# Attention's TensorE work in five pieces a unit from the 17th head on, and the first two weight slices converted in the first batch with GpSimd

## The chip, the cores and the metric

The kernel runs on one core of a Trainium2 chip. The metric is device time of one execution in microseconds (us). The core has TensorE (PE, matmul), VectorE (DVE), ScalarE (ACT), GpSimd (POOL) and SyncE (SP, which issues the DMAs). Each engine works through its own instructions strictly in the order in which they were written, and an instruction whose input is not there holds up all that stand behind it on that engine.

## The reference

Softmax attention with a soft cap over 4 batches of 12 heads (448 tokens, head size 64), then layer norm, a two-layer perceptron (768 to 3072 to 768) and a residual.

```python
scores = cap * np.tanh(scale * np.matmul(q, k.transpose(0, 1, 3, 2)) / cap)   # 4 x 12 heads, 448 x 448
attn = np.exp(scores - np.max(scores, axis=-1, keepdims=True))
attn = attn / (np.sum(attn, axis=-1, keepdims=True) + 1e-09)
x = np.matmul(attn, v)                       # heads side by side: 4 x 448 x 768
xn = (x - mu) / np.sqrt(var + 1e-06) * g_ln
out = x + np.maximum(xn @ w_ch1, 0.0) @ w_ch2   # 768 x 3072, 3072 x 768; weights come as float64
```

## The kernel before

The kernel writes its whole instruction list through a planner of its own. `add` records a piece of work with its engine, a modelled cost, what it reads and writes, and a due time. `emit` then walks a modelled clock: whenever an engine is free in the model, it writes the ready piece with the earliest due time whose buffers are free. The order on each engine is therefore fixed when the program is built, by modelled costs; on the chip only the waits remain.

Attention is done in units of four heads (`quad`, 12 units, two head pairs each). Per unit TensorE has these slots, all in float32: six score slots (L534, two matmuls each: one key tile of 128 for both heads of a pair), one slot for the last 64 keys of all four heads (L545), two slots for the products with v (L428, six matmuls for one pair), one for the last 64 keys' part (L437) and one for the sums of the exponentials (L481, with a column of ones). In the trace each of these matmuls leaves two records. Behind them come transposes of the sums (L493) and of the outputs (L507). ScalarE takes tanh (L558) and exp (L562, L567). VectorE adds up exponentials over key tiles (L413, L415, L420), copies outputs and sums out of PSUM in the first batch (L452; ScalarE does it in the others, L450), forms and multiplies with the reciprocal sums (L496, L499, L517).

The perceptron (FFN) runs over 24 slices of 128 hidden columns. Token tiles are in groups: A0 (3 tiles), A1 (3), then C0 and C1 (8 tiles together), which come last. `up` (L756 to L758) and `down` (L781 to L783) do three float32r matmuls for each product: high by high, high by low, low by high. A0 can begin when the first 12 heads are done and normalized (L651 to L685); from then on TensorE's order mixes FFN matmuls and the attention slots of the units left.

Each slice has two weights, which arrive as float64 bits and are converted in six steps: DMA (L704), exponent scaled into `c` (L709, ScalarE), sign kept in `raw` (L711, GpSimd), two shift-and-or steps (L714, L716, VectorE), rounding into the high part `h` (L364, ScalarE), the low part `l` (L371, VectorE). No conversion begins before `self.late`, the last-keys product (L437) of the second unit. The first two `raw` buffers hold the keys and queries of the first unit before they take weights.

The lines the prediction uses most, beside these: the DMAs of v (L401) and of keys and queries (L387), issued by SP in one order with L704.

Of the kernel before, what the change touches and what calls it, by code (L numbers as in the profile page):

```python
# [66 lines left out]
    w1=20000, w2=3000, evac=2000, cstep=15600, cnorm=10000, load=20000, zpad=3000,  # L67
# [31 lines left out]
class Order:  # L99
# [34 lines left out]
    def emit(self, realize):  # L134
# [29 lines left out]
        while pending:  # L164
            done = False
            for e in free:
# [127 lines left out]
class Program:  # L294
# [79 lines left out]
    def quad(self, i, at):  # L374
# [32 lines left out]
        (self.scores_general if self.general else self.scores)(es, er, kqs, dues)  # L407
# [15 lines left out]
        pos = [buf("ps", "o", [128, 512], F32) for _ in range(2)]  # L423
        for p, e1 in enumerate(es):
            def pv(e, p=p, e1=e1):
                for j in range(NK):
                    for k in range(2):
                        nc.tensor.matmul(pos[p].ap[k * D:k * D + D, :S], lhsT=v.ap[:, (2 * p + k) * NK + j],  # L428
                                         rhs=e1.ap[:, k, j], start=(j == 0), stop=False)

            add({"T": 200 + NK * F4(S)}, pv, reads=[*v_all, (e1, 0), (e1, 1)], writes=[pos[p]], allocs=pos, due=dues[p] - PLAN["pv"])

        def pv_rest(e):
            for k in range(2):
                for p in range(2):
                    rows = slice(p * REST, p * REST + REST)
                    nc.tensor.matmul(pos[p].ap[k * D:k * D + D, :S], lhsT=v.ap[rows, 4 * NK + k],  # L437
                                     rhs=er.ap[rows, k], start=False, stop=True)

        self.last_pv = add({"T": 100 + F4(S)}, pv_rest, reads=[*v_all, er], writes=pos, due=dues[2] - PLAN["pv"])  # L440
# [5 lines left out]
        self.finish(i, ots, s1s, dues[2])  # L446
# [23 lines left out]
    def finish(self, i, pairs, parts, due):  # L470
# [6 lines left out]
        ps = buf("ps", "s", [128, 512], F32)  # L477

        def sums(e):
            for c in range(GROUP):  # L480
                nc.tensor.matmul(ps.ap[32 * c:32 * c + 32, :S], lhsT=self.ones, rhs=parts[c // 2].ap[:, c % 2],  # L481
                                 start=True, stop=True)

        add({"T": 200 + F4(S)}, sums, reads=parts, writes=[ps], due=due)
# [39 lines left out]
    def products(self, kqs, l, r, due, into, allocs):  # L524
# [3 lines left out]
        for p, kq in enumerate(kqs):  # L528
            for j in range(NK):
                zs = [self.buf("ps", "z", [128, 512], F32) for _ in range(2)]  # L530

                def qk(e, j=j, kq=kq, zs=zs):
                    for k, z in enumerate(zs):
                        self.nc.tensor.matmul(z.ap[:, :S], lhsT=kq.ap[rows[k], l, 128 * j:128 * j + 128],  # L534
                                              rhs=kq.ap[rows[k], r], start=True, stop=True)

                self.add({"T": 200 + F4(S)}, qk, reads=[(kq, 0), (kq, 1)], writes=zs, allocs=[allocs[p]], due=due[p] - PLAN["qk"])
                for k, z in enumerate(zs):
                    into(p, k, j, z)
# [383 lines left out]
```

## Time and profile before

| | |
|---|---|
| runs of the kernel before | 931.88, 933.9, 935.34 us; median 933.9 |
| profiled execution | 934.28 us, of which the span of instructions is 932.5 us |
| TensorE busy | 912.0 us of the span, granted clock 0.994 on average |
| VectorE, ScalarE, GpSimd busy | 610.5, 400.5, 134.0 us |
| first FFN matmul | starts 86.49 us into the span |

Times within the profile count from the span's start. PEclk is the granted clock of TensorE as a share of 2.4 GHz. A row of a timeline joins instructions of one line that follow each other; the bracket at its end gives the idle time before it and the instruction that ended that.

### The profile page before, as it was taken

How to read it: one execution, taken by the hardware profiler on the slowest of the kernel's cores; microseconds unless marked ns; L12 is line 12 of the kernel's file. 1: busy time of each engine (PE TensorE's matmuls, PEld its weight loads, DVE VectorE, ACT ScalarE, POOL GpSimd, SP SyncE). 2: the span in 40 equal slices, each digit the busy share in tenths (PEclk: the TensorE clock that was granted, in tenths of full speed). 3: DMA queues.
4: the chain of work that ended last, by engine and by line, in shares of the span. 5: the costliest groups of instructions: out<-in, count | busy, mean ns of one | idle time of the engine just before them, and what ended most of it. 6: DMA issues, size and time to landing. Idle time of an engine off the chain costs nothing.

```text
span 932.5 us, 12642 instructions
## 1 busy us (share of the span) xinstructions
PE 912.0 (98%) x4854; PEld 745.3 (80%) x4854; DVE 610.5 (65%) x900; ACT 400.5 (43%) x569; POOL 134.0 (14%) x224
## 2 busy tenths in 40 slices
PE   8998999899999999999999999999999999999997
PEld 4335766677877778779989998989889889899897
DVE  2698887878777667577898373837483482573622
ACT  6896596765555635653243131212150340330300
POOL 0023211312111101012621010100010120110100
PEclk9999999999999999999999999999999999999999
DMA  4765364444453434227234130402142241250112
GB/s 99 197 176 151 116 187 129 141 136 151 137 159 116 133 92 138 84 86 242 103 100 155 49 129 8 135 1 89 68 166 68 68 167 37 68 179 26 69 52 87
DMA packets 51158, 104.74 MB, mean 112 GB/s; under 512 B 28048, under 2 KB 34704, under 8 KB 51088
## 3 DMA queue, kind: packets, MB, share of 16 engines
q1 hardware_dynamic: 51088, 103.84, 36.2%
q8 instruction: 40, 0.66, 0.3%
q14 instruction: 30, 0.25, 0.1%
HBM read 95.16 MB, written 8.65 MB: 111 GB/s over the span
## 4 chain that ended last, share of the span: by engine, by line
PE 82%; DVE 8%; ACT 2%; POOL 2%; issue 1%; SPq 1%; DMA 1%; DVEq 0%; POOLq 0%; ACTq 0%
PE bank L756 12%; PE bank L781 11%; PE bank L758 11%; PE bank L757 11%; PE bank L783 11%; PE bank L782 11%; PE bank L428 4%; PE bank L534 4%; DVE x L785 2%; DVE raw L714 1%; SPq L401 1%; DVE st L651 1%; PE bank L507 1%; DVE c L716 1%; DVE l L371 1%
## 5 line engine op out<-in xcount | busy, mean ns | idle before, releaser
L781 PE MATMUL bank<-h,hh 128*128 128x384 f32 x672 | 226.0, 336 | 0.3 <-ACT e L558 0.3
L783 PE MATMUL bank<-h,hl 128*128 128x384 f32 x672 | 224.8, 335 | 0.6 <-DVE hl L763 0.6
L782 PE MATMUL bank<-l,hh 128*128 128x384 f32 x672 | 224.6, 334 | 0.0
L785 DVE TENSOR_TENSOR x<-bank,x 128x384 f32<-128x384 f32 x272 | 146.5, 551 | 113.7 <-PE bank L783 112.1
L711 POOL TENSOR_SCALAR raw<-raw 128x768 f32<-128x768 f32 x96 | 98.0, 1022 | 632.3 <-ACT c L709 618.4
L364 ACT ACTIVATE h<-c 128x768 fp32r<-128x768 f32 x96 | 81.0, 846 | 179.7 <-PE bank L783 123.1
L761 ACT ACTIVATE hh<-bank 128x384 fp32r<-128x384 f32 (+1 forms) x96 | 52.3, 545 | 198.7 <-PE bank L758 198.4
L781 PEld LDWEIGHTS bank<-h,hh 128*128 128x128 f32 x672 | 126.1, 188 | 7.9 <-ACT e L558 2.3
L783 PEld LDWEIGHTS bank<-h,hl 128*128 128x128 f32 x672 | 126.1, 188 | 0.9 <-DVE hl L763 0.9
L782 PEld LDWEIGHTS bank<-l,hh 128*128 128x128 f32 x672 | 126.2, 188 | 0.2
L714 DVE SCALAR_TENSOR_TENSOR raw<-raw 128x768 int32<-128x768 int32 x96 | 94.5, 986 | 41.3 <-POOL raw L711 41.0
L709 ACT ACTIVATE c<-raw 128x768 f32<-128x768 f32 x96 | 87.7, 917 | 76.0 <-DVE l L371 37.9
L756 PE MATMUL bank<-hC,h 128*128 128x512 f32 x288 | 114.0, 396 | 0.0
L758 PE MATMUL bank<-hC,l 128*128 128x512 f32 x288 | 113.8, 395 | 0.0
L757 PE MATMUL bank<-lC,h 128*128 128x512 f32 x288 | 113.7, 395 | 0.0
L371 DVE TENSOR_TENSOR l<-c,h 128x768 fp32r<-128x768 f32 x96 | 92.4, 963 | 28.6 <-ACT h L364 28.2
L763 DVE SCALAR_TENSOR_TENSOR hl<-bank,hh 128x384 fp32r<-128x384 f32 (+1 forms) x96 | 59.4, 618 | 67.9 <-ACT hh L761 67.7
L756 PE MATMUL bank<-hA,h 128*128 128x384 f32 x288 | 101.7, 353 | 0.0
L758 PE MATMUL bank<-hA,l 128*128 128x384 f32 x288 | 97.5, 339 | 0.5 <-DVE l L371 0.5
L757 PE MATMUL bank<-lA,h 128*128 128x384 f32 x288 | 97.5, 338 | 0.0
L716 DVE SCALAR_TENSOR_TENSOR c<-c,raw 128x768 int32<-128x768 int32 x96 | 95.0, 991 | 1.9
L558 ACT ACTIVATE e<-bank,sc 128x448 f32<-128x448 f32 x144 | 81.9, 643 | 15.9 <-PE bank L534 15.6
(75 smaller groups left out, 935.2 us busy)
## 6 DMA issues: line engine op xcount, KB each, us to landing
raw<-in_w_dram SPq DMA_DIRECT2D x96, 768.0 KB, 4.4
d<-in_kq_dram SPq DMA_DIRECT2D x44, 224.0 KB, 5.0
out_dram<-x SPq DMA_DIRECT2D x28, 192.0 KB, 1.9
d<-in_v_dram SPq DMA_DIRECT2D x96, 48.0 KB, 3.8
x<-xd SPq DMA_DIRECT2D x8, 384.0 KB, 5.8
xd<-a SPq DMA_DIRECT2D x21, 128.0 KB, 4.5
raw<-in_kq_dram SPq DMA_DIRECT2D x4, 224.0 KB, 4.1
d<-in_v_dram SPq DMA_DIRECT2D x48, 16.0 KB, 2.6
```

Source lines behind the costliest of these rows:

```text
L371: self.eng(e).tensor_tensor(out=out, in0=in_, in1=high.bitcast(F32), op=ALU.subtract)
L709: add({"A": ACTS(DM)}, lambda e: nc.scalar.activation(f(c.ap), f(hi()), AF.Copy, scale=2.0 ** -112), reads=[raw], writes=[c], due=due, aft ...
L711: add(on("sg", G=POOL1(DM), V=VEC1(DM)), lambda e: nc.gpsimd.tensor_scalar(f(hi()), f(hi()), 0.0, 1.0, op0=ALU.mult, op1=ALU.mult) if e == ...
L714: add({"V": VEC2(DM)}, lambda e: nc.vector.scalar_tensor_tensor(hi(), lo(), 29, hi(), op0=ALU.logical_shift_right, op1=ALU.bitwise_or), wr ...
L716: add({"V": VEC2(DM)}, lambda e: nc.vector.scalar_tensor_tensor(c.ap, c.ap, 3, hi(), op0=ALU.logical_shift_left, op1=ALU.bitwise_or), read ...
L756: nc.tensor.matmul(ps.ap[:, :n], lhsT=w1h.ap[:, wc], rhs=xh.ap[:, c], start=(c == 0), stop=False)
L757: nc.tensor.matmul(ps.ap[:, :n], lhsT=w1h.ap[:, wc], rhs=xl.ap[:, c], start=False, stop=False)
L758: nc.tensor.matmul(ps.ap[:, :n], lhsT=w1l.ap[:, wc], rhs=xh.ap[:, c], start=False, stop=(c == CC - 1))
L781: nc.tensor.matmul(o, lhsT=h[0].ap[:, mc], rhs=w[0].ap[:, hc], start=(f == 0), stop=False)
L782: nc.tensor.matmul(o, lhsT=h[0].ap[:, mc], rhs=w[1].ap[:, hc], start=False, stop=False)
L783: nc.tensor.matmul(o, lhsT=h[1].ap[:, mc], rhs=w[0].ap[:, hc], start=False, stop=(f == last))
L785: add({"V": VEC2(HALF)}, lambda e, t=t, ps=ps, hc=hc: nc.vector.tensor_tensor(out=self.x(t)[:, hc], in0=ps.ap[:, :HALF], in1=self.x(t)[:, ...
```

## The change

Three things change. First, from head index 16 on (units 5 to 12) a unit's eleven slots are recorded as five pieces that nothing can be put between: three score pieces of two slots each, one piece of the last-keys slot with the first pair's value product, and one piece of the second pair's value product, the last-keys product and the sums. The first four units keep single slots. The sums' due time is no longer put back by 9 us, in any unit. Second, the first two slices of weights (four conversions) no longer wait for `self.late`, are due 20 us earlier, and have their scaling and rounding (the steps of L709 and L364) on GpSimd, beside the sign step that was there. Third, the planner's model of TensorE's clock counts long pieces over several windows.

```diff
 WEIGHTS = [
-    dict(sg='G', h='A', l='V'),
-    dict(sg='G', h='A', l='V'),
-    dict(sg='G', h='A', l='V'),
+    dict(c='G', sg='G', h='G', l='V'),
+    dict(c='A', sg='G', h='A', l='V'),
 ]
-EARLY = 12
+EARLY = 2
+FINE = 16
 PLAN = dict(
-    ... load=20000, zpad=3000,
+    ... load=20000, zpad=3000, ahead=20000,
 # emit(): the model of TensorE's clock
-                        cold, busy, window = busy < (0.8 if cold else 0.4) * WINDOW, 0.0, window + WINDOW
+                        now = min(busy, WINDOW)
+                        cold, busy, window = now < (0.8 if cold else 0.4) * WINDOW, busy - now, window + WINDOW
 # quad()
-        (self.scores_general if self.general else self.scores)(es, er, kqs, dues)
+        qk_rest = (self.scores_general if self.general else self.scores)(es, er, kqs, dues, 1 if i < FINE else 2)
+        merged = i >= FINE and not self.general
+        if merged:
+            qk_rest(cost, lambda: pv(0), [*v_all, *done(0)], pos)
+        elif not self.general:
+            qk_rest()
...
+        if merged:
+            ps = self.sums(s1s, dues[2], cost + F4(S), lambda: (pv(1), pv_rest()), [*v_all, *done(1), er], pos)
+        else:
+            for p in range(2):
+                add({"T": 200 + cost}, lambda e, p=p: pv(p), reads=[*v_all, *done(p)], writes=[pos[p]],
+                    allocs=pos, due=dues[p] - PLAN["pv"])
+            add({"T": 100 + F4(S)}, lambda e: pv_rest(), reads=[*v_all, er], writes=pos, due=dues[2] - PLAN["pv"])
+            ps = self.sums(s1s, dues[2])
 # sums(), out of finish(): was due=due with PLAN["fin"] added
+            if first:
+                first()
+            for c in range(GROUP):
+                self.nc.tensor.matmul(ps.ap[32 * c:32 * c + 32, :S], lhsT=self.ones, rhs=parts[c // 2].ap[:, c % 2],
+                                      start=True, stop=True)
 # products()
+        slots = [(p, j) for p in range(2) for j in range(NK)]
+        for n in range(0, len(slots), at_once):
+            now = slots[n:n + at_once]
+            zs = [[self.buf("ps", "z", [128, 512], F32) for _ in range(2)] for _ in now]
...
+        def rest(cost=0, then=None, reads=(), writes=()):
...
+                if then:
+                    then()
 # weight()
-        part = WEIGHTS[2 if g else fc >= EARLY]
+        early = g == 0 and fc < EARLY
+        part = WEIGHTS[not early]
+        due -= PLAN["ahead"] * early
...
-        add({"A": ACTS(DM)}, lambda e: nc.scalar.activation(f(c.ap), f(hi()), AF.Copy, scale=2.0 ** -112),
-            reads=[raw], writes=[c], due=due, after=[self.late])
+        add(on("c", A=ACTS(DM), G=POOL1(DM)), lambda e: nc.scalar.activation(
+            f(c.ap), f(hi()), AF.Copy, scale=2.0 ** -112) if e == "A" else nc.gpsimd.tensor_scalar(
+            f(c.ap), f(hi()), 2.0 ** -112, 1.0, op0=ALU.mult, op1=ALU.mult),
+            reads=[raw], writes=[c], due=due, after=[] if early else [self.late])
```

In the order of TensorE, place one is the last unit (heads 45 to 48), amid FFN matmuls. Before, the last-keys product (L437) and the sums (L481) stand apart, and so does L428, just ahead of these rows:

```order
L437 MATMUL bank_208<-d_225,d_288 64x448
L437 MATMUL bank_229<-d_225,d_288 64x448
L437 MATMUL bank_208<-d_225,d_288 64x448
L437 MATMUL bank_229<-d_225,d_288 64x448
L756 MATMUL bank_230<-hA_692,h_67 128x384
L757 MATMUL bank_230<-lA_706,h_67 128x384
L758 MATMUL bank_230<-hA_692,l_69 128x384
L756 MATMUL bank_230<-hA_692,h_67 128x384
L757 MATMUL bank_230<-lA_706,h_67 128x384
L758 MATMUL bank_230<-hA_692,l_69 128x384
L481 MATMUL bank_218<-d_265,ones 32x448 x2
L481 MATMUL bank_218<-d_216,ones 32x448 x2
```

After (L415 is L428 of before, L422 is L437, L491 is L481, L796 to L798 are L756 to L758):

```order
L415 MATMUL bank_208<-e_282,d_270 64x448 x6
L422 MATMUL bank_230<-d_265,d_270 64x448
L422 MATMUL bank_208<-d_265,d_270 64x448
L422 MATMUL bank_230<-d_265,d_270 64x448
L422 MATMUL bank_208<-d_265,d_270 64x448
L491 MATMUL bank_219<-d_323,ones 32x448 x2
L491 MATMUL bank_219<-d_182,ones 32x448 x2
L796 MATMUL bank_200<-hA_1501,h_67 128x384
L797 MATMUL bank_200<-lA_1513,h_67 128x384
L798 MATMUL bank_200<-hA_1501,l_69 128x384
```

The six FFN matmuls that stood between the slots have moved out; the slots follow one another directly.

Place two is VectorE's order in the first unit, behind the last addition of exponentials (`d_248`, `d_288` are the sums of the two pairs; `b_184`, `b_186` take the outputs, `b_190` the sums; `raw` and `c` belong to the weights). Before:

```order
L420 TENSOR_TENSOR d_248<-d_248,d_272 64x896
L420 TENSOR_TENSOR d_288<-d_288,d_272 64x896
L452 COPY b_184<-bank_208 128x448
L452 COPY b_186<-bank_209 128x448
L452 COPY b_190<-bank_229 128x448
L413 TENSOR_TENSOR d_182<-e_282 128x896
L415 TENSOR_TENSOR d_182<-d_182,e_282 128x896
L496 TENSOR_SCALAR r_365<-bank_229,eps 128x16
```

After (L444 is L420, L466 is L452, L754 is L714, L756 is L716, L373 is L371, L437 and L439 are L413 and L415, L515 is L496):

```order
L444 TENSOR_TENSOR d_248<-d_248,d_272 64x896
L444 TENSOR_TENSOR d_288<-d_288,d_272 64x896
L754 SCALAR_TENSOR_TENSOR raw_63<-raw_63 128x768
L466 COPY b_184<-bank_208 128x448
L466 COPY b_186<-bank_209 128x448
L756 SCALAR_TENSOR_TENSOR c_65<-c_65,raw_63 128x768
L466 COPY b_190<-bank_199 128x448
L754 SCALAR_TENSOR_TENSOR raw_64<-raw_64 128x768
L373 TENSOR_TENSOR l_69<-c_65,h_67 128x768
L437 TENSOR_TENSOR d_182<-e_282 128x896
L515 TENSOR_SCALAR r_364<-bank_230,eps 128x16
L439 TENSOR_TENSOR d_182<-d_182,e_282 128x896
```

Two shift-and-or steps of the first weight now stand ahead of the copy into `b_190`, the first of them ahead of all three copies; a step of the second weight and the first low part follow at once.

Place three is TensorE at the same time, from the first unit's sums to the transposes of `b_190`. Before:

```order
L481 MATMUL bank_229<-d_248,ones 32x448 x2
L481 MATMUL bank_229<-d_288,ones 32x448 x2
L428 MATMUL bank_230<-e_282,d_225 64x448 x6
L534 MATMUL bank_209<-d_261 128x448
L534 MATMUL bank_199<-d_261 128x448
L493 MATMUL bank_229<-ident,b_190 128x128 x4
```

After (L512 is L493, L555 is L534):

```order
L491 MATMUL bank_199<-d_248,ones 32x448 x2
L491 MATMUL bank_199<-d_288,ones 32x448 x2
L555 MATMUL bank_200<-d_261 128x448
L555 MATMUL bank_218<-d_261 128x448
L555 MATMUL bank_219<-d_261 128x448
L555 MATMUL bank_229<-d_261 128x448
L512 MATMUL bank_230<-ident,b_190 128x128 x4
L415 MATMUL bank_208<-e_282,d_225 64x448 x6
```

The transposes of `b_190` have moved ahead of the second unit's first value product (L428, now L415).

## Rows read from the trace of the kernel before

**Rows 1.** The page, part 1: busy us (share of the span) xinstructions.

```profile
PE 912.0 (98%) x4854; PEld 745.3 (80%) x4854; DVE 610.5 (65%) x900; ACT 400.5 (43%) x569; POOL 134.0 (14%) x224
```

**Rows 2.** Busy time by stretch: us, each engine busy (x), PEclk, DMA share, GB/s.

```profile
26.22:33.75 7.53, 7.26 (x39) 2.23 (x33) 3.96 (x5) 5.67 (x8) 0.00 (x0) 1.00 1.03 303
33.75:81.27 47.52, 41.30 (x208) 15.49 (x206) 40.40 (x63) 41.94 (x57) 14.17 (x33) 1.00 0.67 165
80.80:84.30 3.50, 2.97 (x14) 2.97 (x15) 3.50 (x5) 2.28 (x4) 0.06 (x1) 0.51 0.80 242
171.60:184.10 12.50, 9.54 (x49) 8.15 (x48) 10.68 (x16) 8.29 (x12) 6.48 (x13) 0.86 0.17 55
200.00:435.00 235.00, 235.00 (x1342) 182.51 (x1341) 168.92 (x246) 131.91 (x192) 29.20 (x40) 1.00 0.42 127
```

**Rows 3.** Timeline of PE in the FFN: start, us, engine, line, operation, count.

```profile
309.50 1.77 PE L534 MATMUL bank<-d 64*128 64x448 f32 x8
...
311.20 0.44 PE L756 MATMUL bank<-hA,h 128*128 128x384 f32 x1
...
312.19 0.34 PE L758 MATMUL bank<-hA,l 128*128 128x384 f32 x1
...
312.46 1.02 PE L534 MATMUL bank<-d 64*128 64x448 f32 x4
...
313.41 0.44 PE L756 MATMUL bank<-hA,h 128*128 128x384 f32 x1
...
313.69 0.34 PE L757 MATMUL bank<-lA,h 128*128 128x384 f32 x1
```

**Rows 4.** Timeline of PE in the first batch, to the first FFN matmul.

```profile
11.77 4.96 PE L428 MATMUL bank<-e,d 128*64 128x448 f32 x12 [1.93 <-ACT e L562]
...
29.50 0.96 PE L481 MATMUL bank<-d,ones 128*32 128x448 f32 x8
...
30.39 2.48 PE L428 MATMUL bank<-e,d 128*64 128x448 f32 x12
...
33.75 0.66 PE L493 MATMUL bank<-ident,b 128*128 128x128 f32 x4
...
81.33 3.36 PE L676 MATMUL bank<-ident,xn 128*128 128x128 f32 x16 [2.65 <-DVE xn L668]
...
86.49 0.44 PE L756 MATMUL bank<-hA,h 128*128 128x384 f32 x1
```

**Rows 5.** Timeline of SP, and line L704 in the window 27.4 to 27.9.

```profile
27.44 0.99 SPq L704 DMA_DIRECT2D raw<-in_w_dram  x2
...
DMA to landing us min/median/max: 6.0/6.0/6.0
```

**Rows 6.** Timeline of DVE in the first batch.

```profile
26.72 1.16 DVE L452 COPY b<-bank 128x448 f32<-128x448 f32 x2 [0.50 <-PE bank L437]
...
62.00 1.62 DVE L714 SCALAR_TENSOR_TENSOR raw<-raw 128x768 int32<-128x768 int32 x1
...
64.94 0.97 DVE L714 SCALAR_TENSOR_TENSOR raw<-raw 128x768 int32<-128x768 int32 x1
...
80.07 1.20 DVE L668 TENSOR_SCALAR xn<-x,mv 128x768 f32<-128x768 f32 x1 [0.91 <-POOL mv L665]
```

**Rows 7.** Timeline of POOL in the first batch.

```profile
61.94 0.88 POOL L711 TENSOR_SCALAR raw<-raw 128x768 f32<-128x768 f32 x1 [3.21 <-ACT c L709]
```

**Rows 8.** Groups by form: line engine op | busy, mean ns | idle before.

```profile
L413 DVE TENSOR_TENSOR d<-e 128x896 f32<-128x896 f32 x24 | 26.0, 1083 | 29.5 <-ACT e L562 29.4
...
L415 DVE TENSOR_TENSOR d<-d,e 128x896 f32<-128x896 f32 x24 | 26.7, 1114 | 0.2
...
L420 DVE TENSOR_TENSOR d<-d,d 64x896 f32<-64x896 f32 x24 | 29.3, 1220 | 7.0 <-ACT d L567 6.6
...
L709 ACT ACTIVATE c<-raw 128x768 f32<-128x768 f32 x96 | 87.7, 917 | 76.0 <-DVE l L371 37.9 <-DMA raw<-in_w_dram 33.1 <-DVE x L785 4.3
...
L364 ACT ACTIVATE h<-c 128x768 fp32r<-128x768 f32 x96 | 81.0, 846 | 179.7 <-PE bank L783 123.1 <-DVE c L716 39.2 <-PE bank L757 17.1
```

More of the change, by code (lines that the diff above doesn't have):

```diff
@@ L421, in quad @@
                 out=s1.ap[rows], in0=s1.ap[rows], in1=er.ap[rows], op=ALU.add), reads=[er], writes=[s1], due=dues[2])
-        ots = []
[L423 to L440, printed above, removed]
+        if merged:
+            ps = self.sums(s1s, dues[2], cost + F4(S), lambda: (pv(1), pv_rest()), [*v_all, *done(1), er], pos)
+        else:
+            for p in range(2):
+                add({"T": 200 + cost}, lambda e, p=p: pv(p), reads=[*v_all, *done(p)], writes=[pos[p]],
+                    allocs=pos, due=dues[p] - PLAN["pv"])
+            add({"T": 100 + F4(S)}, lambda e: pv_rest(), reads=[*v_all, er], writes=pos, due=dues[2] - PLAN["pv"])
+            ps = self.sums(s1s, dues[2])
+        ots = []
         for p in range(2):
@@ L468, in token_tiles, with sums, finish @@
         return [(j, t + j, slice(0, 128) if j else slice(64, 128)) for j in range(4)]
-    def finish(self, i, pairs, parts, due):
+    def sums(self, parts, due, cost=0, first=None, reads=(), writes=()):
+        ps = self.buf("ps", "s", [128, 512], F32)
+        def sums(e):
+            if first:
[3 more added lines that the diff above has]
+                                      start=True, stop=True)
+        self.last_pv = self.add({"T": 200 + F4(S) + cost}, sums, reads=[*parts, *reads], writes=[ps, *writes], due=due)
+        return ps
+    def finish(self, i, pairs, ps, due):
         nc, add, buf = self.nc, self.add, self.buf
@@ L476, in finish @@
         due += PLAN["fin"] if h0 + GROUP < H else 0
[L477 to L484, printed above, removed]
         ss, d0 = self.out_tile("ss", i, due)
@@ L540, in products @@
-        zs = [self.buf("ps", "z", [128, 512], F32) for _ in range(2)]
-        def qk(e):
-            for p, kq in enumerate(kqs):
-                for k, z in enumerate(zs):
-                    self.nc.tensor.matmul(z.ap[p * REST:p * REST + REST, :S], lhsT=kq.ap[rows[k], l, 128 * NK:],
-                                          rhs=kq.ap[rows[k], r], start=True, stop=True)
-        self.add({"T": 200 + F4(S)}, qk, reads=[(kq, k) for kq in kqs for k in range(2)], writes=zs, allocs=[allocs[2]], due=due[2] - PLAN["qk"])
@@ L549, in products, with scores @@
-        for k, z in enumerate(zs):
-            into(2, k, 0, z)
-    def scores(self, es, er, kqs, due):
+                if then:
+                    then()
+            self.add({"T": 200 + F4(S) + cost}, qk, reads=[(kq, k) for kq in kqs for k in range(2)] + list(reads),
+                     writes=[*zs, *writes], allocs=[allocs[2]], due=due[2] - PLAN["qk"])
+            for k, z in enumerate(zs):
+                into(2, k, 0, z)
+        return rest
+    def scores(self, es, er, kqs, due, at_once):
@@ L581, in into @@
                 reads=[z], writes=[tiles[p]], due=due[p])
-        self.products(kqs, 1, 0, due, into, tiles)
+        self.products(kqs, 1, 0, due, into, tiles, at_once)()
         for p, (t, m) in enumerate(zip(tiles, ms)):
```

53 lines of the change are left out of this document (38 added, 15 removed).

## The prediction

> **What bounds the kernel now.** I read the page's shares first, then busy time by stretch, then single rows of TensorE, and from the waits of TensorE back to the engine that it waits for. TensorE is busy for 98% of the span [rows 1]. From 200 to 435 us, where FFN matmuls and attention alternate, it is busy for all 235 us at full clock, while VectorE works 168.9 us and ScalarE 131.9 [rows 2]: there a microsecond less of TensorE is a microsecond less of time, as long as no new wait comes. The first 86.5 us, up to the first FFN matmul [rows 4], are another stage. Between 33.75 and 81.27 us TensorE shows 41.3 of 47.5 us, but part of that is matmuls stretched by waits; ScalarE has 41.9 and VectorE 40.4 us, so VectorE is idle for 7.1 us [rows 2]. The reader should see that three engines share the bound in this stage, and that it ends with the norm of the first tokens: TensorE waits 2.65 us for VectorE's last normalized tile [rows 4], which ends at 80.07 + 1.20 = 81.27 us [rows 6]. The change saves in the second stage and rearranges the first.
>
> **Joining slots: minus 3.9 us.** In the FFN a joined pair of score slots (x8) starts at 309.50 and the next matmul at 311.20: 1.70 us. A lone slot (x4) goes from 312.46 to 313.41: 0.95 us. Joining two therefore saves 2 x 0.95 - 1.70 = 0.20 us. The FFN pays too: from 312.19 the slot's start is 0.27 us away, and the first FFN matmul behind it lasts 0.28 us to the next (313.41 to 313.69), while FFN matmuls follow one another at 0.174 us (from 311.20 to 312.19 there are five such steps, one of 0.28 and four of 0.174). So each stretch of FFN matmuls between two attention slots costs 0.10 + 0.11 = 0.21 us [rows 3]. Now I count in the two orders, from the first FFN matmul on: runs of score slots go from 34 to 23, stretches of FFN matmuls from 57 to 49; runs of the other slots stay as many, since a value product and the sums differ in shape and I let each keep its own start. 11 x 0.20 + 8 x 0.21 = 2.2 + 1.7 = 3.9 us. That is small, because the old order had already joined many slots by chance. The unit's pieces can add waits: a score piece wants four PSUM banks at once and the value product now stands right behind the last-keys slot. The pieces leave at least two FFN stretches between a score piece and its product, and ScalarE has 103 us free of 235 [rows 2], so I cost this at nothing; if the cover is gone, it can eat the 3.9 us, not much more.
>
> **Sums of the fourth unit: minus 0.9 us behind the first FFN matmul.** Their slot takes 30.39 - 29.50 = 0.89 us [rows 4] and moves ahead of it, where a lone score slot leaves its place in the last stretch before the FFN.
>
> **The early weights: plus 6.0 us at the first FFN matmul.** ScalarE is relieved: up to the fourth unit's last exp it loses three scalings of 0.917 and four roundings of 0.846 us [rows 8], 6.1 us in all. ScalarE is only one of three engines here, and the order of VectorE has to be read against SP. SP issues the DMAs of v, keys and queries first, in the same order as before, and reaches the first weight at 27.44 us; it lands 6.0 us later, at 33.4 [rows 5]. Then come two GpSimd steps of about 1 us (0.88 in [rows 7]), so the sign step ends at 35.4. VectorE's first shift-and-or waits for that, and in the new order it stands ahead of the first unit's three copies, which begin at 26.72 before [rows 6]. Behind it now: 0.97 for itself, 1.16 for two copies [rows 6], 0.97 for the second step and 0.6 for the last copy, in all 3.7 us: the copy of the sums ends near 39.0. TensorE's transposes (L493), 33.75 before [rows 4], start at 39.1, and in the new order the second unit's value product stands behind them. TensorE has nothing to do from about 29.5 us on, and ScalarE, which needs the next scores, soon runs dry as well. So the stage is 39.1 - 33.75 = 5.35 us late at this point.
>
> How much returns? From the transposes to the end of the last normalized tile before, VectorE is busy 40.4 us of 47.5 [rows 2]. The new order has the same fourteen weight steps in this stretch, and besides two L413, two L415 and one L420 of VectorE that stood outside: 2 x 1.083 + 2 x 1.114 + 1.220 = 5.6 us by the means [rows 8], 5.1 us when 0.1 each is taken off for their overlap with the next. What VectorE's idle time becomes no row shows: at least none of the 7.1 us, at most all. The tile ends between 39.1 + 40.4 + 5.1 = 84.6 and 91.7 us. I take half, 3.5 us, since the wait for ScalarE shrinks but the waits for transposes and for GpSimd's chain stay: 88.1, or 6.8 us later than 81.27. From there to the first FFN matmul before took 86.49 - 81.27 = 5.2 us, of which 80.8 to 84.3 went at a granted clock of 0.51 after TensorE's wait (1.2 instead of 2.4 GHz) [rows 2]; that half speed costs up to 1.7 us. More work stands close ahead now, so it may be spared; I take half, 0.8. That is +6.0 us, between +1.6 (84.6 and the whole 1.7) and +10.4. The idle 9.6 us also lower the clock at 39 us, as 1.93 idle us did before the value product that took 4.96 us where another takes 2.48 [rows 4]; this falls within the idle time counted.
>
> Does less conversion remain afterwards? At the first FFN matmul the same four low parts are done as before, so no slice comes earlier relative to TensorE.
>
> **The second norm: minus 1.9 us.** Around the second norm of 3 tiles, 171.6 to 184.1 us, TensorE is idle for 12.5 - 9.5 = 3.0 us and its mean clock is 0.86, which is another 1.7 [rows 2]. Between the last output transposes and the norm's the old order has 21 FFN matmuls, three lone score slots and a value product: 21 x 0.174 + 3 x 0.95 + 2.4 + 0.4 for the edges = 9.3 us. The new one has 33 FFN matmuls, a joined pair, a last-keys slot (taken as long as the sums) and a value product: 5.7 + 1.7 + 0.9 + 2.4 + 0.5 = 11.2 us. The 1.9 us more cover as much of the wait. Bounds: nothing, or all 4.7 us. The third norm and the end keep their order nearly unchanged: nothing.
>
> **Sum.** On the profiled execution: 934.3 + 6.0 - 0.9 - 3.9 - 1.9 = 933.6 us. This execution stands 0.4 us above the median of 933.9, which I leave out as smaller than the rest. I predict 934 us. The likeliest case by itself spans 930 to 938.
>
> **A rule that speaks against the change.** The row first: a GpSimd sign step ran from 61.94 to 62.82 [rows 7], and the VectorE step that started at 62.00 took 1.62 us instead of 0.97 [rows 6], 0.65 more. The Trainium skill, "SBUF — State Buffer", section "Who interferes with whom", says that VectorE with two SBUF inputs and a GpSimd instruction that reads SBUF exclude each other for a whole instruction. The trace agrees, with 0.65 us; by that rule eight more GpSimd steps in a busy VectorE stage would make the slower case below.
>
> **Rivals.**
> 1. *GpSimd holds VectorE up in the first batch: slower.* Eight added GpSimd steps fall between 33 and 56 us, where VectorE is now the fullest engine. If each costs it 0.65 us [rows 6, 7], the stage loses 5.2 us more: 6.0 + 5.2 = 11.2, and the time is 934.3 + 11.2 - 6.7 = 938.8, or 941 if more of VectorE's idle time stays than the half I took. For it: the pair of rows, and that low parts wait for GpSimd's rounding. Against: in many cases it is GpSimd that waits, and its chain has slack. It decides from a first FFN matmul at 97.5 us on (86.5 + 11.0, by which the sum passes 938.6).
> 2. *VectorE fills all its idle time: faster.* Then the first FFN matmul is 1.6 us late, and with 1.9 to 4.7 us from the second norm the time is 934.3 + 1.6 - 0.9 - 3.9 - 1.9 = 929.2 down to 926.4; I put 928. For it: ScalarE is relieved by 6.1 us, and it ended most of VectorE's idle time at L413 [rows 8]. Against: at the end of the stage the norm's chain through GpSimd leaves VectorE waiting in any order (0.91 us before its last tile [rows 6]).
> 3. *The change does not do what it says:* joined pieces stand together but TensorE waits within them for banks or exp, and the 3.9 us go into waits: 934.3 + 6.0 - 0.9 - 1.9 = 937.5.
>
> **How the numbers follow.** Likeliest case 0.54, rival 1 0.20, rival 2 0.18, rival 3 0.08. A measurement of this kernel can tell about 0.5% from no change, that is 4.7 us: faster is below 929.2, slower above 938.6. Rival 2 lies below (0.18) with 0.03 from the likeliest case; rival 1 lies above with 0.03 from the likeliest case and 0.03 from rival 3: faster 0.21, same 0.53, slower 0.26. The range reaches to both outer rivals: 927 to 941.
>
> **What would show it.** Right: TensorE waits some 9 us for VectorE's copy ahead of the first unit's L493 transposes, near 30 to 39 us; VectorE stands idle from 26 to 35 us until GpSimd's first sign step; the first FFN matmul at 90 to 95 us; from then on TensorE's record free of new waits, with score pieces of 1.70 us. Wrong: a first weight that lands well before 33 us; a first FFN matmul ahead of 86.5 us, which would give the early weights their gain; or value products with waits of a microsecond in the FFN stage.

## The result and the profile after

| | before | after |
|---|---|---|
| median of the runs taken together | 933.46 us | 942.94 us |
| profiled execution | 934.28 us | 943.18 us |
| its span of instructions | 932.5 us | 941.3 us |
| first FFN matmul starts | 86.49 us | 97.17 us |
| from there to the last matmul's end | 840.7 us | 836.9 us |
| from VectorE's last result to the end of the span | 4.7 us | 6.7 us |

The changed kernel is slower: ratio 1.010, 95% interval 1.0081 to 1.0120. The forecast was 934 with a range of 927 to 941, and the likeliest case was no change. The table splits the 8.8 us between the two spans: +10.7 up to the first FFN matmul, -3.9 from there to the last matmul, +2.0 behind it. TensorE's busy time in the middle part fell by 5.7 us, and its idle time rose by 1.9 (before, then after; us, then busy us of PE, PEld, DVE, ACT, POOL, then granted clock, DMA share, GB/s):

```profile
86.49:927.21 840.72, 836.27 (x4496) 712.77 (x4494) 552.43 (x808) 331.28 (x472) 118.52 (x178) 1.00 0.34 108
```

```profile
97.17:934.02 836.85, 830.54 (x4490) 712.13 (x4486) 546.03 (x806) 332.58 (x474) 118.61 (x178) 1.00 0.34 107
```

TensorE in the first batch of the changed kernel (start, us, line, operation, count, idle time before and what ended it), the answer to [rows 4]:

```profile
27.90 1.77 PE L555 MATMUL bank<-d 64*128 64x448 f32 x8
39.64 1.09 PE L512 MATMUL bank<-ident,b 128*128 128x128 f32 x4 [9.96 <-DVE b L466]
40.66 4.18 PE L415 MATMUL bank<-e,d 128*64 128x448 f32 x12
...
93.13 0.66 PE L712 MATMUL bank<-ident,xn 128*128 128x128 f32 x4 [1.50 <-DVE xn L704]
...
97.17 0.45 PE L796 MATMUL bank<-hA,h 128*128 128x384 f32 x1
```

The wait of 9.96 us ahead of the transposes (L512, L493 before) is the one that the prediction described. GpSimd's first two steps and VectorE behind them:

```profile
33.66 0.87 POOL L748 TENSOR_SCALAR c<-raw 128x768 f32<-128x768 f32 x1 [28.20 <-DMA raw<-in_w_dram]
34.62 0.86 POOL L751 TENSOR_SCALAR raw<-raw 128x768 f32<-128x768 f32 x1
```

```profile
35.51 0.96 DVE L754 SCALAR_TENSOR_TENSOR raw<-raw 128x768 int32<-128x768 int32 x1 [8.83 <-POOL raw L751]
...
38.88 0.61 DVE L466 COPY b<-bank 128x448 f32<-128x448 f32 x1
...
47.17 1.41 DVE L536 TENSOR_TENSOR x<-bank,r 128x256 f32<-128x256 f32 x4 [2.50 <-PE bank L526]
...
92.39 0.68 DVE L704 TENSOR_SCALAR xn<-x,mv 128x768 f32<-128x768 f32 x1 [0.65 <-POOL mv L701]
```

The weight lands at 33.5 us, the sign step ends at 35.5, the copy of the sums at 39.5. ScalarE, whose next scores stand behind the transposes on TensorE, runs dry in turn:

```profile
45.83 1.16 ACT L589 ACTIVATE e<-bank,sc 128x448 f32<-128x448 f32 x2 [13.47 <-PE bank L555]
```

Stretches of the changed kernel (us, then busy us of PE, PEld, DVE, ACT, POOL, then granted clock): the 10 us around the end of the wait, the stage from the transposes to the last normalized tile, and the second norm, which answers to the fourth row of [rows 2].

```profile
33.90:44.10 10.20, 4.46 (x14) 1.95 (x16) 8.59 (x12) 0.00 (x0) 5.02 (x7) 0.50 0.56 146
39.64:93.07 53.43, 46.59 (x226) 17.54 (x226) 46.18 (x67) 35.50 (x48) 22.49 (x37) 0.93 0.64 170
186.00:198.50 12.50, 9.66 (x60) 6.18 (x59) 11.14 (x16) 7.89 (x14) 4.01 (x11) 1.00 0.26 79
```

After the wait TensorE runs at 1.2 instead of 2.4 GHz (0.50), so the value product at 40.66 takes 4.18 us; before, the one at 30.39 took 2.48. The second norm runs at full clock, with 2.8 us idle.

What VectorE waited for in this stage (us in total, times, longest), after and then before:

```profile
DVE x L536 <- PE bank L526: 3.0, 2, 2.5
DVE xn L704 <- POOL mv L701: 1.6, 2, 0.9
DVE d L437 <- ACT e L593: 1.5, 1, 1.5
DVE l L373 <- POOL h L370: 0.7, 1, 0.7
```

```profile
DVE raw L714 <- POOL raw L711: 2.1, 2, 1.3
DVE xn L668 <- POOL mv L665: 1.6, 2, 0.9
DVE r L496 <- PE bank L493: 1.0, 1, 1.0
DVE x L517 <- PE bank L507: 0.8, 1, 0.8
```

The old waits for the sign steps (2.1 us) went, but waits for TensorE and ScalarE came: 6.8 us of waits in all, against 7.1 us of idle time before [rows 2]. In the FFN one new stall appears in this profile, a transfer that lands late and holds ScalarE's copies, for which TensorE waits:

```profile
144.87 0.90 ACT L747 ACTIVATE c<-raw 128x768 f32<-128x768 f32 x1 [4.10 <-DMA raw<-in_w_dram]
```

```profile
147.21 0.63 PE L512 MATMUL bank<-ident,b 128*128 128x128 f32 x4 [1.62 <-ACT b L464]
```

That load (issued at 136.12 behind another weight, keys and queries) took 8.7 us to land; the median of such loads is 4.5. The stall is not in every execution: in a second profile of the changed kernel (told below) the load took 7.3 us, TensorE's wait of 1.62 us is absent, and the stretch from the first FFN matmul to the last took 835.1 us.

### The profile page after: what moved, and what is told of

It is laid out like the page before. It is cut to its first block, busy times and chain, and to the rows that moved or that the text cites. A ratio compares the mean times of both kernels' runs of the same rounds, so it can differ in the third digit from the quotient of the medians.

```text
span 941.3 us, 12620 instructions
## 1 busy us (share of the span) xinstructions
PE 906.6 (96%) x4854; PEld 744.4 (79%) x4854; DVE 608.1 (65%) x900; ACT 394.8 (42%) x561; POOL 146.9 (16%) x232
## 4 chain that ended last, share of the span: by engine, by line
PE 84%; DVE 7%; ACT 3%; DMA 2%; POOL 2%; issue 1%; SPq 0%; DVEq 0%; POOLq 0%; ACTq 0%
PE bank L796 12%; PE bank L821 12%; PE bank L798 12%; PE bank L797 11%; PE bank L823 11%; PE bank L822 11%; PE bank L415 5%; PE bank L555 4%; DMA raw<-in_w_dram 1%; ACT e L593 1%; PE bank L491 1%; DVE x L825 1%; DVE c L756 1%; PE bank L422 1%; DVE raw L754 1%
## 5 line engine op out<-in xcount | busy, mean ns | idle before, releaser
L366 ACT ACTIVATE h<-c 128x768 fp32r<-128x768 f32 x92 | 77.5, 846 | 170.0 <-PE bank L823 110.9
L754 DVE SCALAR_TENSOR_TENSOR raw<-raw 128x768 int32<-128x768 int32 x96 | 93.0, 969 | 58.8 <-POOL raw L751 58.6
L747 ACT ACTIVATE c<-raw 128x768 f32<-128x768 f32 x92 | 83.9, 912 | 87.4 <-DVE l L373 45.5
L796 PE MATMUL bank<-hC,h 128*128 128x512 f32 x288 | 114.0, 396 | 0.0
L798 PE MATMUL bank<-hC,l 128*128 128x512 f32 x288 | 113.8, 395 | 0.0
L373 DVE TENSOR_TENSOR l<-c,h 128x768 fp32r<-128x768 f32 x96 | 92.3, 961 | 29.2 <-ACT h L366 28.1
L796 PE MATMUL bank<-hA,h 128*128 128x384 f32 x288 | 100.6, 349 | 0.0
L756 DVE SCALAR_TENSOR_TENSOR c<-c,raw 128x768 int32<-128x768 int32 x96 | 96.0, 1000 | 3.2 <-ACT h L366 0.5
L798 PE MATMUL bank<-hA,l 128*128 128x384 f32 x288 | 97.1, 337 | 0.4 <-DVE l L373 0.4
```

What stands on the lines that cost most here:

```text
L373: self.eng(e).tensor_tensor(out=out, in0=in_, in1=high.bitcast(F32), op=ALU.subtract)
L747: add(on("c", A=ACTS(DM), G=POOL1(DM)), lambda e: nc.scalar.activation(f(c.ap), f(hi()), AF.Copy, scale=2.0 ** -112) if e == "A" else nc.g ...
L754: add({"V": VEC2(DM)}, lambda e: nc.vector.scalar_tensor_tensor(hi(), lo(), 29, hi(), op0=ALU.logical_shift_right, op1=ALU.bitwise_or), wr ...
L756: add({"V": VEC2(DM)}, lambda e: nc.vector.scalar_tensor_tensor(c.ap, c.ap, 3, hi(), op0=ALU.logical_shift_left, op1=ALU.bitwise_or), read ...
L796: nc.tensor.matmul(ps.ap[:, :n], lhsT=w1h.ap[:, wc], rhs=xh.ap[:, c], start=(c == 0), stop=False)
L798: nc.tensor.matmul(ps.ap[:, :n], lhsT=w1l.ap[:, wc], rhs=xh.ap[:, c], start=False, stop=(c == CC - 1))
```

## The experiments

Theory 1 was that the early steps stand on VectorE ahead of copies that TensorE wants and wait there for a transfer that lands late. Theory 2 is the first rival, GpSimd's steps that lengthen VectorE's. Theory 3 is on the pieces (at first, that they cost what they save; in a later run, that they do save 4 to 5 us and lose them elsewhere). Theories 4 and 5 came from the runs and are told where they came up. A first FFN matmul read from a single profile is uncertain by 1 to 3.5 us (the changed kernel: 97.17 and 98.46; the kernel before: 86.49, and 90.03 in a run with the same order of instructions), so times are compared by their ratios and profiles by their rows.

**The two parts apart.** `EARLY = 0` leaves the pieces without early weights, `FINE = 48` (slots single to the end) the early weights without pieces. Both keep the rest of the change, that is, the sums' earlier due time and the new model of the clock.

```diff
-EARLY = 2
+EARLY = 0          # e1
-FINE = 16
+FINE = 48          # e2
```

> The five pieces alone; the weights are converted as before the change. Theory 1 (VectorE waits in its order for the first weight, which lands at 33 us): the 10 us wait ahead of the first unit's sum transposes is gone, the first FFN matmul stands at 84 to 88 us, and the time is 933.5 - 4.8 (slots and sums) with 0 to 3 us of new waits: 928 to 932. Theory 2 (GpSimd holds VectorE up): the same. Theory 3 (pieces that ask for four PSUM banks at once cost what they save): 935 to 943.

935.39 us, ratio 1.0017 (1.0001 to 1.0033), in the range of theory 3: the pieces gain nothing. From the first FFN matmul to the last it was 836.25 us, 4.5 less than before; but that matmul came at 89.62, 3.1 later than before, and 7.1 us instead of 5.3 followed the last one.

> The early weights alone; every unit keeps single slots. Theories 1 and 2: the wait of about 10 us is there, the first FFN matmul at 95 to 98 us, and the time 942 to 946, since little of the slots' gain is left. Theory 3: 932 to 936.

943.54 us, ratio 1.0098 (1.0071 to 1.0125), first FFN matmul at 98.22: the loss belongs to the early weights. From there to the last matmul it took 837.5 us, 3.3 less than before though every slot is single: the fourth unit's sums and two score slots had moved ahead of the first FFN matmul. So a shorter stretch is not by itself a gain of the pieces.

**The weight landed earlier.**

```diff
-nc.sync.dma_start(out=raw..., in_=src[fc]...)
+(nc.scalar if early and w == 0 else nc.sync).dma_start(out=raw..., in_=src[fc]...)
```

> The changed kernel, but the DMAs of the first two weights are issued by ScalarE at its place after 13 tanh and 2 exp (near 19 us) and not by SP at 27.7. Theory 1: they land near 24 us, VectorE's wait of 8.8 us goes, the transposes start by 32 us, the first FFN matmul stands at 82 to 88 us, time 927 to 934. Theory 2: the transposes start early, but the GpSimd steps beside VectorE stay, so the first FFN matmul stands at 91 us or later and the time is 937 or more.

936.58 us, ratio 1.0023 (1.0010 to 1.0037): 6.4 us less than the changed kernel, with the pieces and every conversion step kept. So the late landing, with what queues behind it, is a large part of the loss, but not all: the transposes started at 36.41 and the first FFN matmul at 93.23, where theory 1 had expected 32 and 82 to 88. One reason is that ScalarE stood idle ahead of its second load:

```profile
18.91 0.38 ACTq L743 DMA_DIRECT2D raw<-in_w_dram  x1
19.34 1.41 ACT L593 ACTIVATE e<-e,capt 128x1344 f32<-128x1344 f32 x1 [0.20 <-ACT e L589]
24.89 0.33 ACTq L743 DMA_DIRECT2D raw<-in_w_dram  x1
25.27 1.42 ACT L593 ACTIVATE e<-e,capt 128x1344 f32<-128x1344 f32 x1 [4.51 <-DMA d<-in_v_dram]
```

As the last row's bracket says, the issue waited for another transfer: a load of v, which SP had issued at 19.20 and which landed at 24.82.

**GpSimd beside VectorE.** Eight copies of 768 columns added on GpSimd in the first two units of the kernel before:

```diff
+for k in range(2 if i < 2 * GROUP else 0):
+    nc.gpsimd.tensor_scalar(scr, e1[:, k, :768], 1.0, 1.0, op0=ALU.mult, op1=ALU.mult)
 nc.vector.tensor_tensor(out=s1.ap, in0=e1.ap[:, :, 0], in1=e1.ap[:, :, 1], op=ALU.add)
```

> The kernel before, with eight more GpSimd steps of 768 columns in the first two units (a copy of exponentials into a tile that nobody reads), each started by the same exp as VectorE's additions and beside them. Nothing waits for them but GpSimd's own queue. Theory 1: the collision alone costs the first FFN matmul 0 to 2 us, time 933 to 936. Theory 2: eight times 0.65 us, first FFN matmul near 91.5 us, time 938 to 939.

933.56 us, ratio 0.9989 (0.9974 to 1.0004). I took this at first for the end of the second theory, but it is inconclusive: in its trace three of the eight copies lengthened a VectorE step (1.60, 1.59 and 1.59 instead of 1.09 us, at 13.32, 21.03 and 40.43), 1.5 us in all, in a kernel whose VectorE has idle time there. In the changed kernel six VectorE steps beside a GpSimd step took 0.3 to 0.7 us more than others of their kind, 3.3 us in all; before, three (1.5 us). GpSimd pays too: six of its conversion steps took 1.6 to 3.7 us there, most others 0.8 to 0.9. The next two runs ask in the changed kernel itself.

```diff
-... if e == "A" else nc.gpsimd.tensor_scalar(f(c.ap), ...            # scaling
+... if early and fc and w or e == "A" else nc.gpsimd.tensor_scalar(f(c.ap), ...
-lambda e: self.round(e, h.ap, f(c.ap))
+lambda e: self.round("A" if early else e, h.ap, f(c.ap))             # e9
-reads=[raw], writes=[c], due=due, after=[] if early else [self.late])
+reads=[raw], writes=[c], due=due, after=[self.late])                 # e8
```

> Same order as the changed kernel, but the four roundings and one scaling of the early weights are issued by ScalarE at the same places of the program, so GpSimd loses five of its steps in the first batch. Theory 2: the lengthened VectorE steps (0.5 to 0.7 us each beside a GpSimd step) shrink by 2 to 3 us and so does the time: 940 to 941. Theory 1: the wait of 10 us ahead of the first transposes stays, VectorE's lengthened steps lay partly in idle time, and the time stays at 942 to 944; ScalarE's 4.3 us more of work fall into its idle time.

940.50 us, ratio 1.0069 (1.0052 to 1.0086), as the second theory said; but the wait of 10 us stayed (10.16) and the first FFN matmul moved by only 0.5 us (96.69). The median is 2.4 us below the changed kernel's; by the ratios to the kernel before it is 1.7 us below a repetition of the changed kernel (1.0087, further down). The intervals overlap, so a gain is likely but not shown. VectorE's busy time in the stage fell from 46.18 to 44.61 us:

```profile
39.90:92.60 52.70, 47.64 (x226) 17.02 (x226) 44.61 (x67) 40.61 (x57) 14.65 (x32) 0.91 0.65 171
```

> The first two slices keep their GpSimd scalings and roundings but, as in the kernel before, may not begin before the point self.late. Theory 1 (the steps stand on VectorE ahead of copies that TensorE wants, and wait there for a transfer that lands at 33.5 us): TensorE no longer waits 10 us ahead of the first transposes of the sums, the first FFN matmul starts at 87 to 91 us instead of 97.2, and the time is 932 to 937 us. Theory 2 (GpSimd's steps lengthen VectorE's wherever they stand): VectorE still has some 3 us of lengthened steps, the first FFN matmul starts at 93 to 96 us, and the time is 938 to 942.

939.71 us, ratio 1.0059 (1.0043 to 1.0076); first FFN matmul at 94.59. The wait of 10 us is gone (transposes at 29.30), and still that matmul is 8.1 us later than before, 5.0 later than with pieces alone, as theory 2 said. Eight VectorE steps are lengthened here by 4.1 us in all, and VectorE waits for GpSimd's sign steps with evacuations (L536) behind the waiting step, for which TensorE waits:

```profile
59.34 0.96 DVE L754 SCALAR_TENSOR_TENSOR raw<-raw 128x768 int32<-128x768 int32 x1 [1.75 <-POOL raw L751]
60.21 0.42 DVE L536 TENSOR_TENSOR x<-bank,r 128x256 f32<-128x256 f32 x1
```

```profile
60.69 1.77 PE L555 MATMUL bank<-d 64*128 64x448 f32 x6 [1.81 <-DVE x L536]
```

So the first theory does not hold alone: the conversion through GpSimd costs the first batch time where it stands late, too. (This run also keeps the early weights' due time, 20 us ahead; the two were not separated.)

**The clock.** Idle-filling matmuls ahead of the transposes that wait:

```diff
+for j in range(40 if i == 0 else 0):       # 60 in the first try
+    nc.tensor.matmul(pr.ap[:, :128], lhsT=self.ident, rhs=self.ident, start=True, stop=True)
 for j in range(NK + 1):
     nc.tensor.transpose(...)
```

> The changed kernel with 60 idle-filling matmuls of 128x128 ahead of the first transposes of the sums, where TensorE waits 10 us; they compute nothing that is used. Theory 1 with the clock as a part of the loss: the granted clock stays at full from 34 to 44 us, the value product at 40.7 us takes 2.5 instead of 4.2 us, and up to 2 us come back: 941 to 942.5. If VectorE alone bounds the stage, the faster matmuls end in waits for VectorE and the time stays at 943.

944.28 us: each matmul went as two passes, so they held TensorE until 42.8 us, 3.2 too long, and the end came only 1.3 later.

> As the run with 60 idle-filling matmuls, of which each went as two passes of 0.114 us so that they held TensorE until 42.8 us; with 40 they end near 38.5 us, before the copy that TensorE waits for (39.6). The clock stays at full: value product 2.5 instead of 4.2 us. If the clock has a part in the loss: first FFN matmul at 95.5 to 96.5 us and 941.2 to 942.3. If VectorE alone bounds the stage: 97.2 us and 943.

941.29 us, ratio 1.0069 (1.0046 to 1.0092), which overlaps the changed kernel's. So both were run again on one chip:

> The changed kernel itself, unaltered, beside the run with forty matmuls, so that the two share the runs of the kernel before: 942 to 944, first FFN matmul near 97 us.

> The forty idle-filling matmuls again, beside the changed kernel. If the lower clock behind the wait of 10 us is a part of the loss: first FFN matmul 1.4 to 1.8 us earlier than in the run beside it and 1 to 2 us less time. If not: no difference beyond 0.5 us.

The changed kernel took 942.60, the one with forty matmuls 940.95 (ratios 1.0087, 1.0069 to 1.0105, and 1.0078, 1.0059 to 1.0097); in the two profiles the first FFN matmul moved from 98.46 to 96.25, with the copy that the transposes wait for at the same place (in the first pair, from 97.17 to 95.60). By the profiles the clock costs about 2 us; the times agree in sign, their intervals overlap. The matmuls, the wait and the value product at full clock:

```profile
29.62 9.20 PE L512 MATMUL bank<-ident 128*128 128x128 f32 x80
39.70 0.66 PE L514 MATMUL bank<-ident,b 128*128 128x128 f32 x4 [0.88 <-DVE b L466]
40.29 2.48 PE L415 MATMUL bank<-e,d 128*64 128x448 f32 x12
```

**The pieces behind the old first batch.** No early weights; sums of the first four units recorded late, with their old due time, the old model of the clock, and `self.late` back on the last-keys product (in the changed kernel it has moved on to the sums).

```diff
-EARLY = 2
+EARLY = 0
-ps = self.sums(s1s, dues[2])
+ps = None        # recorded behind the copies:
+ps = self.sums(s1s, dues[2] + (PLAN["fin"] if i % H + GROUP < H else 0))
```

> Pieces from the 17th head on, no early weights, and the first four units recorded as before (sums recorded late with their old due time, the old model of the clock), so that the first batch has nearly the old order. Theory 3 (the pieces do save 4 to 5 us from the first FFN matmul on, and the run with pieces alone lost them in the first batch, 3.1 us, and at the program's end, 1.8 us): first FFN matmul at 86 to 88 us, 836 us from there to the last matmul, and 928 to 931 us in all. Rival (the pieces bring waits of their own): 933 to 935, with new waits between the first FFN matmul and the last.

937.89 us, ratio 1.0038 (1.0023 to 1.0052): my expectation failed. The first FFN matmul came at 86.76 as hoped, but 842.6 us followed. Between 160 and 190 us TensorE stands idle for 30 - 22.78 = 7.2 us, ahead of transposes of the sums (3.42), an FFN matmul (0.78) and the second norm's transposes (2.8), and its granted clock is 0.89. That the pieces stand elsewhere relative to the loads is the likely reason; it was not tested. What the pieces save is of the size of what one shift of the order costs in such stalls.

**The end of SP's program.** In the changed kernel, SP's closing instructions show a gap of 1.87 us behind the last store's landing; in the kernel before there is none. The gap stands behind the 544th to 547th SP instruction in every kernel that has it; in those that have none, the wait for the last store stands there or later. The ten profiles with the gap show 31 packets of instructions on queue q14, the ten without it 30, and in the changed kernel one of these packets starts at 938.40, within the gap (938.26 to 940.13). Theory 4 is that SP waits there for its own next instructions. Eight loads of 4 bytes to each partition were added far ahead of the end:

```diff
+self.spare = self.tile("spare", [128, 1])
+if g and w and 8 <= fc < 16:
+    nc.sync.dma_start(out=self.spare, in_=cap.partition_broadcast(128))
```

> The changed kernel with eight more tiny loads (4 bytes to each partition, never used) in SP's program, far ahead of the end, so that SP's closing instructions stand 8 to 16 places later. Theory 4 (at the end SP waits 1.8 us for its next block of instructions, which in the kernel before was fetched while SP waited for the last store): the gap between two of SP's closing instructions goes, the time from the last VectorE instruction to the end falls from 6.7 to 4.5 to 5 us, and the time is 941.0 to 941.5. Rival (the end is longer because the last store lands later or varies from run to run): 943.

934.42 us, ratio 1.0006 (0.9994 to 1.0018). The end fell to 4.9 us as expected, but 8.5 us went, not 1.8.

> Pieces without early weights, and SP's end moved as in the run beside it. Theory 4: 935.4 - 1.8 = 933.6 (933 to 934), level with the kernel before: what is left of the pieces' 4.5 us is then eaten in the first batch, where 1.6 us of TensorE's work was moved and 1.5 us of new waits came. Rival: 935.4.

927.40 us, ratio 0.9941 (0.9919 to 0.9963).

> The changed kernel with three repairs: the first weight's load alone issued by ScalarE (where both were, ScalarE stood 5.5 us ahead of the second issue), roundings and one scaling of the early weights by ScalarE, and SP's end moved as in the run beside it. Theory 1 and 2 together: first weight's sign step ends near 26 instead of 35.5 us, TensorE's transposes of the first sums start near 34 to 36 us at the latest, the first FFN matmul at 90 to 92 us; 835.5 from there, 5.3 behind the last matmul: 930.5 to 934. If the second weight's late landing (35.8 us) sets the stage anyway: 935 to 938.

927.98 us, ratio 0.9926 (0.9902 to 0.9950). Both came out below what was expected (933 to 934, and 930.5 to 934). In all three the last groups' first-layer matmuls had become faster. The new tile had moved the tiles behind it by 32 bytes, among them those of the weights (`h`, `l`), but not `hC` and `lC`, which these matmuls stream against the weights: by the addresses in the built programs they start at the same place in all kernels. To separate this, the kernel before got the tile without the loads, and the three kernels got a tile of 64 bytes:

```diff
+self.spare = self.tile("spare", [128, 1])       # e14: kernel before, nothing else
-self.spare = self.tile("spare", [128, 1])       # e11b, e12b, e13b
+self.spare = self.tile("spare", [128, 16])
```

> The kernel before with one more tile of 4 bytes in each partition, never used, ahead of the others, by which every later tile starts 32 bytes further on; no instruction is added. Theory 5 (with the tiles 32 bytes further on, the first-layer matmuls of the last groups run faster: 144 in 32.65 instead of 33.60 us and 108 in 22.70 instead of 23.05, as in the three runs that had such a tile): 4 x 0.95 + 3 x 0.35 + 0.3 = 5.2 us less, 928 to 929.5. Rival (the gain of those runs came from the loads in SP's program): 933 to 934.5.

928.47 us, ratio 0.9935 (0.9918 to 0.9953). The group of these matmuls from 520 us on (count | busy us, mean ns), in the kernel before and then moved by 32 bytes:

```profile
L756 PE MATMUL bank<-hC,h 128*128 128x512 f32 x264 | 104.3, 395 | 0.0
```

```profile
L757 PE MATMUL bank<-hC,h 128*128 128x512 f32 x264 | 102.7, 389 | 0.0
```

Three such groups give 3 x 1.6 = 4.8 of the 5.9 us between the medians.

> The changed kernel with the eight tiny loads in SP's program, but into a tile of 64 bytes, so that the other tiles move by 64 bytes. Theory 4 and 5 together (32 bytes gave the matmuls, the loads only the end): first-layer matmuls at 33.60 for 144 again, the time behind VectorE's last instruction 4.7 to 5.2 instead of 6.7 us, 940.5 to 941.5. Rival (the loads gave all): 934.5.

940.42 us, ratio 1.0066 (1.0048 to 1.0084); the end takes 4.4 us, the matmuls are slow again (395 ns). VectorE's last result in the changed kernel (span 941.3 us) and its packets of instructions:

```profile
934.06 0.56 DVE L825 TENSOR_TENSOR x<-bank,x 128x384 f32<-128x384 f32 x1 [1.53 <-PE bank L823]
```

```profile
q14 instruction: 31, 0.25, 0.1%
```

The same in this run (span 938.5 us); the kernel before has 30 packets, too:

```profile
933.55 0.56 DVE L831 TENSOR_TENSOR x<-bank,x 128x384 f32<-128x384 f32 x1 [1.53 <-PE bank L829]
```

```profile
q14 instruction: 30, 0.25, 0.1%
```

> First load by ScalarE, roundings and one scaling by ScalarE, SP's end moved, tiles moved by 64 bytes: what the three repairs give without the faster matmuls. Theory 1, 2 and 4: 928.0 + 5.2 = 933 to 934, level with the kernel before, so that the early weights' loss of 10 us and the end's 1.8 us are all returned but the change brings nothing. Rival (the matmuls' share is smaller): 930 to 932.

933.86 us, ratio 0.9990 (0.9973 to 1.0007).

> Pieces without early weights, SP's end moved, tiles moved by 64 bytes: what the pieces alone bring. Theory 3 and 4: 935.4 - 1.8 = 933.6 down to 927.4 + 5.2 = 932.6; a gain of the pieces of at most 1.5 us over the kernel before. Rival (pieces' 4 to 5 us come through): 929 to 930.

934.69 us, ratio 1.0009 (0.9990 to 1.0027).

Both are level with the kernel before. With the first load on time, GpSimd relieved and SP's end repaired, the early weights lose nothing, and neither part gains anything that can be measured. With the pieces alone the joining does show in TensorE's busy time from the first FFN matmul on, 831.6 instead of 836.3 us, but the idle time there rose by 2.2 us and the first FFN matmul came 1.6 later. With the three repairs that matmul still came at 91.71, 5.2 later than before, and the stretch behind it was 5.3 shorter. Three versions beat both kernels (927.4, 928.0 and 928.5 us); what they have in common is the shift by 32 bytes, not the change. In the kernel with the load by ScalarE (tiles at 64 bytes) the transposes of the first sums wait 0.90 us, not 9.96:

```profile
30.91 0.63 PE L514 MATMUL bank<-ident,b 128*128 128x128 f32 x4 [0.90 <-DVE b L468]
31.47 2.48 PE L417 MATMUL bank<-e,d 128*64 128x448 f32 x12
```

## Why the prediction was wrong

The mechanism of the largest term was right and its size wrong. The sum on record was 933.6; three terms miss the profiled 943.2 by 4.7, 2.8 and 2.0 us.

**Early weights: +6.0 predicted, +10.7 measured.** The steps up to the transposes held: 39.1 forecast, 39.64 measured. From there, VectorE's work was put at 45.5 us and was 46.18. The step that failed is "I take half" of VectorE's idle time, 3.5 us: 53.43 - 46.18 = 7.25 us of the stage stayed idle. I reasoned that the wait for ScalarE would shrink; it is 1.5 us, where before there were two waits for it of 0.5 and 0.6. The longest new wait, 2.50 us for TensorE's transposes (L526), stands behind the value product at half clock. The last part, 97.17 - 93.07 = 4.1 us, was put at 4.4. So the measured 10.7 lies just beyond the upper bound of +10.4 (and the second profile's 12.0 well beyond it); the mean of two bounds was no estimate. Not all of it is the early weights': without them the three runs with pieces in the new order have their first FFN matmul at 88.1 to 89.6, 1.6 to 3.1 us later than before, and with the first four units' sums recorded as before it stands at 86.8. The prediction put nothing for this reordering of the first batch.

The prediction also said that the lower clock behind the idle 9.6 us "falls within the idle time counted". It did not: holding the clock moved the first FFN matmul by 2.2 us in one pair of profiles and 1.6 in the other.

**Slots, sums and second norm: -6.7 predicted, -3.9 measured.** TensorE's busy time in this stretch fell by 5.7 us. Slots and sums were put at -4.8, and 1.7 us of low clock at the second norm went, so about 4.0 of the 4.8 came. The second norm's -1.9 came out by luck: the prediction let more work cover the wait, but the wait hardly shrank, from 3.0 to 12.50 - 9.66 = 2.8 us; what went is the low clock. The step that failed is "I cost this at nothing": 2.5 us of new waits (1.62, 0.38 and 0.49) came between 147 and 151 us, of which the load that landed in 8.7 us is the start. It was ScalarE's copies behind a weight's scaling, not the pieces' banks, that TensorE waited for. In the second profile the 1.62 is absent and the stretch is 5.6 us shorter than before, so this miss is between 1.1 and 2.8 us. These waits differ with every order, as the run with the old first batch showed with 7.2 us of them.

**The end: 0 predicted, +2.0 measured.** The step that failed is that the end keeps its order "nearly unchanged: nothing". SP's program lost three instructions, and its last instructions, fetched under the wait for the last store before, now come behind it: 1.87 us. The Trainium skill, "Runtime: NRT & Kernel Launch", section "Instruction fetch mechanics", calls the cost of a block boundary "mostly hidden"; at the end of this program, where SP had nothing else left to do, it was not.

**Rivals.** The first, GpSimd holding VectorE up, named 938.8 to 941 and a first FFN matmul from 97.5 us on. The first FFN matmul stands at 97.17 and 98.46 in the two profiles, so its sign was met in one, and the time lies beyond its 941. Its price is real but was not the cause alone: taking five GpSimd steps away gave 1.7 to 2.4 us in time, with overlapping intervals, and left the wait of 10 us. The Trainium skill's rule that was weighed ("SBUF — State Buffer", "Who interferes with whom") agrees with the six lengthened steps: a VectorE step that starts beside a GpSimd step waits for about what is left of that, 0.3 to 0.7 us. Eight GpSimd steps in the kernel before met VectorE's three times, and no time was lost. The second rival's condition, that VectorE fills its idle time, is the opposite of what happened. The third, waits within the pieces, was not seen; the pieces ran in 1.77 us.

Not settled: how the early weights' 10.7 us divide exactly between the landing, the clock and GpSimd, since each repair also moves the others (6.4, about 2, and 1.7 to 2.4 us in time), and which part of GpSimd's share lies in the first batch.

## What to carry to other kernels

A step that is moved ahead in an in-order engine brings its transfer's landing with it: read when the load lands by the queue that issues it, and if the step then waits, count the idle time of every engine that feeds back into it, in full, and the clock behind it. When work is relabelled rather than removed, a gain of 0.5% is smaller than what a reordering gives or takes elsewhere, so count the whole span, its end included. And test an accidental side of an experiment: an unused tile of 4 bytes was worth more than the change.

## What the runs showed of the hardware

- An unused tile of 4 bytes, which moves the tiles of the weights by 32 bytes, made matmuls with 512 columns take 389 instead of 395 ns on average, 4.8 us from 520 us on; one of 64 bytes changed nothing (395). By the addresses in the built programs, the weights (`h`, `l`) start at a multiple of 64 bytes in the slow case and 32 past one in the fast case, while `hC` and `lC` start 32 past one in both. That this is the cause was not tried beyond the two shifts.
- SP can wait 1.3 to 2.0 us for its own instructions at the end of a program, depending on how many instructions stand ahead.
- Beside VectorE steps, GpSimd steps on 768 columns took 1.6 to 3.7 us (six in the changed kernel's first batch) where most others took 0.8 to 0.9, and VectorE steps beside them 0.3 to 0.7 us more.
